# Another order for the first loads, the row products and the early FFN units of a causal attention and FFN kernel

## The chip, the cores and the metric

The kernel runs on one core of a Trainium2 chip. The metric is the device time of one execution in microseconds (us); lower is better. Engines: PE (TensorE), DVE (VectorE), ACT (ScalarE), POOL (GpSimd) and SP (SyncE), each with its own queue of instructions, which it works off in order. DMA transfers are issued from the queues of SP and POOL.

## The reference

Causal attention with 16 beacon keys that every query sees (8 batches, 8 heads, 576 tokens, head size 64), and on its output a multiplicative FFN with four weights.

```python
k_all = concat([beacon_k, k], axis=2); v_all = concat([beacon_v, v], axis=2)
scores = q @ k_all^T / sqrt(64)          # later tokens masked, beacons never
a = softmax(scores); x = (a @ v_all)     # -> 4608 tokens x 512
out = (((x @ w1) * (x @ w2)) @ w3) @ w_out      # d_ff = 1024
```

Inputs and output are float32.

## The kernel before, in words

All matmuls are in float16. `w3 @ w_out` is formed once, on the chip, into `Wt` (8 row blocks of 128 by 512), so the FFN is two matmul stages. The instructions stand in the order in which the program writes them; a framework adds the semaphores. A tile pool with `bufs=n` hands out n buffers in turn, and a new tile waits until all that used the old one in its buffer is done. On POOL's and on SP's queue a DMA also waits for the DMA that was issued eight before it on that queue.

**The head.** `load_first(a)` issues on SP, for a = 0 to 3, row block a of w3 and the matching 256 rows of w_out as float32 into a staging tile of pool `gp` (two buffers); `cast_first` turns them to float16, w3 on DVE and w_out on ACT. `w3_transposed(kt)` turns block kt on PE (8 transposes) and copies the result on DVE (`wT`). `fuse(acc, wT, r0, r1)` multiplies it with pieces r0 to r1 of w_out into an accumulator; pieces 2a and 2a+1 come from w_out load a. The accumulators of blocks 0 to 3 lie in the two `ps` tiles that the attention scores use afterwards. Blocks 4 to 7 follow in between the attention of batch 0: `row_first` (transposes), `row_a`, `row_b` (four fuses each) and a copy to `Wt` on ACT or DVE. `spin(n)` issues n matmuls on zeros.

**Loads.** `later_loads()` puts the other loads on POOL's queue, with a cast to float16 on the way: `load_pair(t)` (q and k of two heads of batch 0), `load_w3(4..7)`, `load_v(0, c)` (v of batch 0 in 5 chunks and the beacons), `load_w12` (w1 and w2), then q, k and v of batch 1. A memset on DVE at L144 comes ahead of the first of them, and the queue waits for it. `reorder_first(t)` (DVE) and `pe_transpose_first(t)` (PE, then DVE and ACT copies) make qT and kT of pair t, here T(t). Batch 1 is transposed on PE as well (`pe_transpose_second`). From batch 2 on, `transpose_qk(b, c)` does it by DMA transposes on SP, one for q and one for k of each of 5 chunks.

**Attention.** A step s is half of a head pair; 8 steps make a batch (`NSB`). `ahead(s)` is `scores(s)` and its two exps. `scores(s)` fills two `ps` tiles (pool `psS`, two buffers), `exps(s, j)` empties them on ACT, `masks` runs on DVE, `values(s)` multiplies with v, and DVE writes the normalised x. Batch 0 and 1 are put into `xT` by PE transposes (`pe_transpose_x`), later batches by DMA transposes on SP.

**The FFN** is a stream of units, one matmul of 128x512 each. A token tile of 512 has 96 units: 64 of `ff_ab` (groups of four; the first group of a pair is copied by ACT to `a_sb`, the second is multiplied with it by DVE) and 32 of `ff_out` (DVE, then a store on SP). `emit_ff(n)` puts n units into PE's queue. `marks` says how many units are out by which step:

```python
    for s in range(NSB, NS):
        ...
        values(s)
        ...
        k1 = min(4, fill[s])
        emit_ff(k1)
        if more:
            exps(s + 1, 1)
            mask(s + 1, 0)
        emit_ff(fill[s] - k1)
```

Here `scores(s + 1)` and `exps(s + 1, 0)` come ahead of `values(s)`, so that the second exp stands behind the first k1 units in the program.

Of the kernel before, what the change touches and what calls it, by code (L numbers as in the profile page):

```python
# [8 lines left out]
FP32 = mybir.dt.float32  # L9
# [3 lines left out]
ds, ts = bass.ds, bass.ts  # L13
# [26 lines left out]
def kernel(  # L40
# [13 lines left out]
    nc = tc.nc  # L54
# [78 lines left out]
    def load_pair(t):  # L133
        o16s[t] = []
        for i, (src, home) in enumerate(((q, q16s), (k, k16s))):

            flat = (
                home[0].rearrange("p c d -> p (c d)")[:NR, ds(t * RUN * P, RUN * P)]
                if t < 2
                else xT[:NR, 2 * (t - 2) + i, ds(2 * S, RUN * P)]  # L140
            )
            st = flat.rearrange("p (h x) -> p h x", h=2)
            if t == 0 and i == 0:
                nc.vector.memset(st[0:1, 0, 0:1], 0.0)  # L144
            nc.gpsimd.dma_start(
                st, src[0, ds(2 * t, 2)].rearrange("h (p j) d -> p h (j d)", j=RUN)
            )
            o16s[t].append(st)
        if t == 0:
            nc.gpsimd.dma_start(  # L150
                b16.rearrange("p (h d) -> p h d", h=H),
                beacon_k[0].rearrange("h n d -> n h d"),
            )
# [3 lines left out]
    def reorder_first(t):  # L157
        for i in range(2):
            o16 = tiny.tile([P, RUN, P], FP16, name=f"o16_{i}")
            nc.vector.tensor_copy(  # L160
                o16[:NR].rearrange("p j (h d) -> p h j d", h=2),
                o16s[t][i].rearrange("p h (j d) -> p h j d", j=RUN),
            )
            o16s[t][i] = o16

    def pe_transpose_first(t):
        qT, kT = qTs[0], kTs[0]
        for o16, dst, off, copy in (
            (o16s[t][0], qT, 0, nc.vector.tensor_copy),
            (o16s[t][1], kT, Nb, nc.scalar.copy),  # L170
        ):
            pt = psM.tile([P, 1024], FP16, name="pm")
            for j in range(RUN):
                nc.tensor.transpose(pt[:, ds(j * NR, NR)], o16[:NR, j, :], ident[:NR, :NR])
            if off:
                nc.tensor.transpose(pt[:, ds(S, Nb)], b16[:, ts(t, P)], ident[:Nb, :Nb])
                copy(dst[:, t, 0:Nb], pt[:, ds(S, Nb)])
            copy(
                dst[:, t, ds(off, S)].rearrange("p (i j) -> p i j", j=RUN),
                pt[:, 0:S].rearrange("p (j i) -> p i j", j=RUN),  # L180
            )
# [34 lines left out]
    def spin(n):  # L216
        pm = psM.tile([P, 512], FP32, name="pm")
        for _ in range(n):
            nc.tensor.matmul(pm, zeros[:, 0:P], zeros)  # L219
# [15 lines left out]
    def load_w3(kt):  # L235
        nc.gpsimd.dma_start(w316[:, kt // 2, kt % 2], moe_w3[ts(kt, P), :])
# [6 lines left out]
            )  # L243


    firsts = []

    def load_first(a):
        st = gp.tile([P, 2, 2 * DM], FP32, name="gT")
        nc.sync.dma_start(st[:, 0, :], moe_w3[ts(a, P), :])  # L250
        nc.sync.dma_start(
            st[:, 1, :],
            moe_w_out[ds(a * 2 * P, 2 * P), :].rearrange("(p c) n -> p (c n)", c=2),
        )
        firsts.append(st)

    def cast_first(a, i):
        if i == 0:
            nc.vector.tensor_copy(w316[:, a // 2, a % 2], firsts[a][:, 0, :])
        else:  # L260
            nc.scalar.copy(
                wo16[:, ds(2 * a, 2), :].rearrange("p c n -> p (c n)"), firsts[a][:, 1, :]
            )

    load_first(0)
    load_first(1)
    nc.gpsimd.affine_select(
        ident,
        ident,
# [25 lines left out]
    def later_loads():  # L295
        load_pair(0)
        load_w3(4)
        load_pair(1)
        load_w3(5)
        for c in range(NJT):  # L300
            load_v(0, c)
        load_pair(2)
        load_w3(6)
        load_pair(3)
        load_w3(7)
        load_w12(0)
        load_w12(1)
        for c in range(NJT):
            load_q(1, c)
            load_k(1, c)  # L310
        for c in range(NJT):
            load_v(1, c)


    def w3_transposed(kt):
        pt = psM.tile([P, NFT, P], FP16, name="pm")
        for rt in range(NFT):
            nc.tensor.transpose(
                pt[:, rt, :],
                w316[:, kt // 2, kt % 2, ds((rt // 2) * 2 * P, 2 * P)].rearrange(  # L320
                    "p (x c) -> p c x", c=2
                )[:, rt % 2, :],
                ident,
            )
        wT = wp.tile([P, NFT, P], FP16, name="wT")
        nc.vector.tensor_copy(wT, pt)  # L326
        return wT

    def fuse(acc, wT, r0, r1):
        for rt in range(r0, r1):  # L330
            nc.tensor.matmul(  # L331
                acc,
                wT[:, rt, :],
                wo16[:, rt, :],
                start=(rt == 0),
                stop=(rt == NFT - 1),
            )
# [51 lines left out]
    def emit_ff(n):  # L389
        nonlocal emitted  # L390
        for _ in range(n):
            try:
                next(ff)
            except StopIteration:
                return
            emitted += 1
# [83 lines left out]
    n_first = 4  # L480
    fill = [0] * NS

    marks = [(NSB, 52), (2 * NSB, 96), (2 * NSB, 104), (26, 196), (58, 580), (NS, 652)]
    for (s0, u0), (s1, u1) in zip(marks, marks[1:]):
        for s in range(s0, s1):
            n = s1 - s0
# [2 lines left out]
    def ahead(s):  # L489
        scores(s)  # L490
        for j in range(2):
            exps(s, j)

    def masks(s):
        for j in range(2):
            mask(s, j)
# [4 lines left out]
    grow = [psS.tile([P, 2, 512], FP32, name="ps") for _ in range(2)]  # L501
    accs = [grow[kt // 2][:, kt % 2, :] for kt in range(4)]
    wTs = []
    for a in range(4):
        cast_first(a, 0)
        wTs.append(w3_transposed(a))
        cast_first(a, 1)
        if a < 2:
            load_first(a + 2)
        if a == 1:  # L510
            later_loads()
        if a:
            for kt in range(a):
                fuse(accs[kt], wTs[kt], 2 * a - 2, 2 * a)
            spin(1)
            fuse(accs[a], wTs[a], 0, 2 * a)
        else:
            spin(5)
    for kt in range(4):
        fuse(accs[kt], wTs[kt], NFT - 2, NFT)  # L520
    reorder_first(0)
    for kt in range(4):
        copy = nc.vector.tensor_copy if kt % 2 else nc.scalar.copy
        copy(Wt[:, kt, :], accs[kt])

    rows = {}

    def row_first(kt):
        wT = w3_transposed(kt)
        rows[kt] = (wT, psM.tile([P, DM], FP32, name="pm"))  # L530

    def row_a(kt):
        fuse(rows[kt][1], rows[kt][0], 0, 4)

    def row_b(kt):
        fuse(rows[kt][1], rows[kt][0], 4, NFT)
        copy = nc.scalar.copy if kt < 6 else nc.vector.tensor_copy
        copy(Wt[:, kt, :], rows[kt][1])

    pe_transpose_first(0)  # L540
    spin(3)
    ahead(0)
    reorder_first(1)
    pe_transpose_first(1)
    row_first(4)
    ahead(1)
    row_a(4)
    masks(0)
    ahead(2)
    reorder_first(2)  # L550
    pe_transpose_first(2)
    row_b(4)
    masks(1)
    row_first(5)
    ahead(3)
    row_a(5)
    masks(2)
    values(0)
    ahead(4)
    reorder_first(3)  # L560
    pe_transpose_first(3)
    row_b(5)
    masks(3)
    values(1)
    row_first(6)
    ahead(5)
    row_a(6)
    values(2)
    masks(4)
    ahead(6)  # L570
    for c in range(NJT):
        load_q(2, c)
        load_k(2, c)
    row_b(6)
    values(3)
    masks(5)
    row_first(7)
    ahead(7)
    values(4)
    masks(6)  # L580
    row_a(7)
    values(5)
    row_b(7)
    values(6)
# [2 lines left out]
    for c in range(NJT):  # L587
        load_v(2, c)
    pe_transpose_x(0)
    emit_ff(40)  # L590
    pe_transpose_second(0)
    emit_ff(4)
    pe_transpose_second(1)
# [4 lines left out]
    for s in range(NSB, NS):  # L598
        b, r = s // NSB, s % NSB
        more = s + 1 < NS and s + 1 != 2 * NSB  # L600
        if more:
            scores(s + 1)
            exps(s + 1, 0)
        values(s)
        if b == 1 and r % 2 == 0 and r < NSB - 4:
            pe_transpose_second(r // 2 + 2)
# [7 lines that stand above are left out]
            mask(s + 1, 1)  # L614
        if s == 2 * NSB - 1:
            pe_transpose_x(1)
            ahead(s + 1)
            emit_ff(8)
            masks(s + 1)
        if 1 <= b < B - 1:  # L620
            if r == (0 if b > 1 else 3):
                for c in range(NJT if b > 1 else 0):
                    load_v(b + 1, c)
                for c in range(NJT if b + 2 < B else 0):
                    load_q(b + 2, c)
                    load_k(b + 2, c)
            if 1 <= r <= NJT:
                transpose_qk(b + 1, r - 1)
    emit_ff(1 << 30)
# [28 lines left out]
```

## Time and profile before

| | |
|---|---|
| median of 6 runs | 317.92 us (315.68 to 323.82) |
| profiled execution | 317.32 us, span 315.6 us |
| clock of TensorE | 1.00 of full speed |
| PE busy | 293.8 us, 93% of the span |
| DVE, ACT, POOL busy | 165.6, 160.0, 114.8 us |
| first FFN matmul | 49.73 us after the span's start |

The span runs from the first to the last instruction; the time has some 1.7 us around it. In the profile's lines L12 is line 12 of the kernel; a group reads engine, operation, output <- input. A line of the list of waits reads: engine, tile and line that waited <- what ended the wait: us in total, times, longest. A line in order of time reads: start, duration (first to last of a run of alike instructions), engine, line, operation, shape, count, and in brackets the idle time ahead of it with its releaser.

### The profile page before, as it was taken

What the parts mean: (1) busy time and instruction counts of PE and PEld (TensorE: products, weight loads), DVE (VectorE), ACT (ScalarE), POOL (GpSimd) and SP (SyncE); (2) the same over time, 40 slices, a digit from 0 to 9 for tenths busy, and PEclk for the clock granted to TensorE, in tenths of its full rate; (3) what the DMA queues carried; (4) which work ended last, traced back from release to release, by engine and by line L of the source; (5) the groups of instructions that cost most, each with busy time, mean ns of one, the idle gap of its engine ahead of it and who ended that gap; (6) DMA issues with size and microseconds to landing.
All of it is one profiled execution on the core that took longest, in us unless ns stands there. A gap on an engine that the chain in (4) does not pass through costs nothing.

```text
span 315.6 us, 6971 instructions
## 1 busy us (share of the span) xinstructions
PE 293.8 (93%) x2813; PEld 150.6 (48%) x2813; DVE 165.6 (52%) x383; ACT 160.0 (51%) x225; POOL 114.8 (36%) x155
## 2 busy tenths in 40 slices
PE   8897878989879997999999999999999999999995
PEld 3353554445535453555554555455455554444442
DVE  4554674446635663556555555555555554434342
ACT  2347733476457763664566456745655661230320
POOL 4669359939484149306910871050000000000000
PEclk9999999999999999999999999999999999999999
DMA  7999999999999999999999999998434003402003
GB/s 261 305 169 184 205 160 131 119 155 90 144 216 141 157 114 158 184 140 116 205 168 145 118 226 154 135 120 187 92 67 134 28 2 67 143 0 100 33 2 133
DMA packets 162048, 42.67 MB, mean 135 GB/s; under 512 B 152288, under 2 KB 155872, under 8 KB 162016
## 3 DMA queue, kind: packets, MB, share of 16 engines
q0 software_dynamic: 109792, 17.57, 78.5%
q1 hardware_dynamic: 52224, 24.66, 40.6%
q8 instruction: 22, 0.36, 0.5%
q14 instruction: 10, 0.08, 0.1%
HBM read 39.32 MB, written 9.44 MB: 154 GB/s over the span
## 4 chain that ended last, share of the span: by engine, by line
PE 68%; DMA 17%; POOL 5%; DVE 4%; issue 3%; ACT 2%; SPq 0%; DVEq 0%; POOLq 0%
PE pm L346 33%; PE pm L367 14%; PE pv L454 9%; PE ps L412 6%; DMA k<-in_k_dram 5%; DMA qT<-q 3%; DMA xT<-in_moe_w_dram 3%; DMA xT<-x 2%; DMA kT<-k 2%; PE pm L331 2%; PE pm L219 2%; POOL q L103 1%; DMA xT<-in_k_dram 1%; ACT pT L421 1%; DVE wT L326 1%
## 5 line engine op out<-in xcount | busy, mean ns | idle before, releaser
L346 PE MATMUL pm<-xT,w 128*128 128x512 f16 x576 | 132.1, 379 | 2.8 <-DMA xT<-x 2.1
L421 ACT ACTIVATE pT<-ps 128x736 f16<-128x736 f32 (+3 forms) x128 | 105.3, 864 | 38.3 <-PE ps L412 37.9
L346 PEld LDWEIGHTS <-w 128*128 128x128 f16 x576 | 53.8, 98 | 62.6 <-issue 3.9
L357 ACT ACTIVATE a_sb<-pm 128x512 f32<-128x512 f32 x72 | 43.0, 597 | 79.3 <-PE pm L346 78.9
L359 DVE TENSOR_TENSOR gT<-pm,a_sb 128x512 f16<-128x512 f32 x72 | 49.8, 692 | 52.0 <-PE pm L346 51.9
L367 PE MATMUL pm<-Wt,gT 128*128 128x512 f16 x288 | 66.2, 379 | 0.1
L112 POOL DMA_DIRECT2D va<-in_v_dram x40 | 33.9, 860 | 58.5 <-PE pv L454 55.7
L454 PE MATMUL pv<-va,pT 128*128 128x65 f16 x912 | 41.3, 194 | 1.6 <-DVE pT L433 1.5
L454 PEld LDWEIGHTS <-pT 128*128 128x128 f16 x960 | 34.3, 97 | 14.3 <-issue 5.4
L412 PE MATMUL ps<-qT,kT 64*128 64x80 f16 (+3 forms) x704 | 36.2, 228 | 5.0 <-DMA qT<-q 1.6
L367 PEld LDWEIGHTS <-gT 128*128 128x128 f16 x288 | 26.7, 98 | 29.1 <-issue 0.4
L462 DVE RECIPROCAL rd<-pv 128x4 f32<-128x4 f32 (+1 forms) x62 | 11.7, 189 | 49.7 <-PE pv L454 49.6
L377 DVE TENSOR_SCALAR ot<-pm 128x512 f32<-128x512 f32 x36 | 24.9, 691 | 23.0 <-PE pm L367 22.9
L103 POOL DMA_DIRECT2D q<-in_q_dram x35 | 30.4, 870 | 16.6 <-DMA k<-in_k_dram 4.3
L412 PEld LDWEIGHTS <-kT 64*128 64x128 f16 x704 | 20.6, 95 | 32.2 <-issue 27.4
L112 POOL DMA_DIRECT2D k<-in_k_dram x35 | 30.3, 865 | 9.8 <-DMA q<-in_q_dram 4.4
L463 DVE TENSOR_TENSOR x<-pv,rd 128x256 f16<-128x256 f32 (+1 forms) x62 | 30.3, 489 | 2.4
L433 DVE TENSOR_TENSOR pT<-pT,MB 128x512 f16<-128x512 f16 x64 | 20.1, 324 | 0.2 <-ACT pT L421 0.2
L433 DVE TENSOR_TENSOR pT<-pT,MA 128x480 f16<-128x480 f16 x32 | 12.8, 399 | 0.3 <-ACT pT L421 0.3
L219 PE MATMUL pm<-zeros 128*128 128x512 f16 x25 | 9.0, 502 | 1.3 <-DVE zeros L214 1.3
L331 PE MATMUL pm<-wo,wT 128*128 128x512 f16 x32 | 8.3, 381 | 1.8 <-DVE wT L326 1.7
L331 PEld LDWEIGHTS <-wT 128*128 128x128 f16 x64 | 5.4, 98 | 7.9 <-DVE wT L326 2.5
(62 smaller groups left out, 104.1 us busy)
## 6 DMA issues: line engine op xcount, KB each, us to landing
out_dram<-ot SPq DMA_DIRECT2D x36, 256.0 KB, 4.0
q<-in_q_dram POOLq DMA_DIRECT2D x28, 128.0 KB, 10.3
va<-in_v_dram POOLq DMA_DIRECT2D x24, 128.0 KB, 6.2
k<-in_k_dram POOLq DMA_DIRECT2D x21, 128.0 KB, 11.5
gT<-in_moe_w_dram SPq DMA_DIRECT2D x4, 512.0 KB, 3.6
gT<-in_moe_w_out_dram SPq DMA_DIRECT2D x4, 512.0 KB, 4.4
w<-in_moe_w_dram POOLq DMA_DIRECT2D x4, 512.0 KB, 11.2
xT<-in_moe_w_dram POOLq DMA_DIRECT2D x4, 256.0 KB, 6.3
```

The costliest lines, as they stand in the source:

```text
L103: nc.gpsimd.dma_start(q16s[b % NB2][:rows, c, :].rearrange("s (h d) -> s h d", h=H), q[b, :, ds(c * P, rows), :].rearrange("h s d -> s h d"),)
L112: nc.gpsimd.dma_start(dst[ds(p0, rows)], src[b, :, ds(s0, rows), :].rearrange("h s d -> s h d"))
L346: nc.tensor.matmul(pm, w12[:, kt, ds(i * DF + kf * P, P)], xT[:, kt, ds(mc * 512, 512)], start=(kt == 0), stop=(kt == NKT - 1),)
L357: nc.scalar.activation(a_sb, pm, AF.Copy, scale=GS)
L359: nc.vector.tensor_tensor(gT[:, kf, :], pm, a_sb, ALU.mult)
L367: nc.tensor.matmul(pm, gT[:, kf, ts(mt, P)], Wt[:, kf, :], start=(kf == 0), stop=(kf == NFT - 1),)
L377: nc.vector.tensor_scalar(ot, pm, float(1.0 / GS), None, ALU.mult)
L412: nc.tensor.matmul(ps[:, hh, ds(col, n)], kT[ds(hh * 64, 64), t, ts(jt, P)], qT[ds(hh * 64, 64), t, ds(q0, n)],)
L421: nc.scalar.activation(pT[:, :, ds(GO[g], GW[g])], pss[s][j][:, :, 0 : GW[g]], AF.Exp, scale=scale)
L433: nc.vector.tensor_tensor(blk, blk, m.unsqueeze(1).to_broadcast([P, 2, n]), ALU.mult)
L454: nc.tensor.matmul(pv[:, 2 * n + hh, 0:65], pT[:, hh, ds(col, P)], va[:, jt, 2 * t + hh, 0:65], start=(jn == 0), stop=(jn == len(BLK[i]) - 1),
L463: nc.vector.tensor_tensor(x16[:, ds(tiles[0], ni), ds(t * P, P)].rearrange("p i (h d) -> p i h d", h=2), pv[:, 0 : 2 * ni, 0:64].rearrange ...
```

## The change

- The first loads and casts are ordered w3(0), w_out(0), w3(1), w_out(1), w3(2), w3(3), w_out(2), w_out(3). A staging tile holds two w3 blocks or two w_out blocks, not one of each. The cast of a w_out load is shared: one half on ACT, one on DVE. Fuses and spins are ordered accordingly, and pair 0's transposes stand ahead of the last eight fuses.
- In `later_loads`, batch 0's v loads go behind pair 2, and the seventh w3 block behind pair 3.
- The row products of batch 0 stand in another order; `row_first` is now `row_t`, with the accumulator taken in `row_a`; the copies of blocks 4 to 6 are on DVE and that of block 7 is on ACT.
- Ahead of batch 1 there are 52 FFN units, not 40; the marks are 64 units (52 before) at step 8 and 192 at step 27 (196 at step 26).
- The ten DMA transposes of batch 2 are queued on SP right after those 52 units, ahead of any store; before, they were queued in steps 9 to 13, with a store after the second chunk and after the fourth.

```diff
+    firsts = {}
+    def load_first(i, a):
+        if a % 2 == 0 and i == 0:
+            firsts[a // 2] = [gp.tile([P, 2, 2 * DM], FP32, name="gT") for _ in range(2)]
+        st = firsts[a // 2][i][:, a % 2, :]
         ...
+    def cast_first(i, a):
+        st = firsts[a // 2][i][:, a % 2, :]
+        if i == 0:
+            nc.vector.tensor_copy(w316[:, a // 2, a % 2], st)
+        else:
+            nc.scalar.copy(wo16[:, 2 * a, :], st[:, 0:DM])
+            nc.vector.tensor_copy(wo16[:, 2 * a + 1, :], st[:, DM:])
+    for a in range(2):
+        for i in range(2):
+            load_first(i, a)
     ...
         load_w3(5)
+        load_pair(2)
         for c in range(NJT):
             load_v(0, c)
-        load_pair(2)
+        load_pair(3)
         load_w3(6)
-        load_pair(3)
         load_w3(7)
     ...
-    marks = [(NSB, 52), (2 * NSB, 96), (2 * NSB, 104), (26, 196), (58, 580), (NS, 652)]
+    marks = [(NSB, 64), (2 * NSB, 96), (2 * NSB, 104), (27, 192), (58, 580), (NS, 652)]
     ...
+    cast_first(0, 0)
+    wTs.append(w3_transposed(0))
+    spin(5)
+    cast_first(1, 0)
+    cast_first(0, 1)
+    load_first(0, 2)
+    load_first(0, 3)
+    wTs.append(w3_transposed(1))
+    fuse(accs[0], wTs[0], 0, 2)
+    spin(1)
+    cast_first(1, 1)
+    load_first(1, 2)
+    load_first(1, 3)
+    later_loads()
+    fuse(accs[1], wTs[1], 0, 2)
+    fuse(accs[0], wTs[0], 2, 4)
+    fuse(accs[1], wTs[1], 2, 4)
+    for a in (2, 3):
+        cast_first(0, a)
+        wTs.append(w3_transposed(a))
+        spin(3)
+        fuse(accs[a], wTs[a], 0, 4)
+    for a in (2, 3):
+        cast_first(1, a)
+        if a == 3:
+            reorder_first(0)
+            pe_transpose_first(0)
+        for kt in range(4):
+            fuse(accs[kt], wTs[kt], 2 * a, 2 * a + 2)
     ...                              # copies of accs to Wt, as before
+    ahead(0); reorder_first(1); pe_transpose_first(1)
+    row_t(4); ahead(1); row_a(4); masks(0); ahead(2); row_b(4); masks(1)
+    row_t(5); reorder_first(2); pe_transpose_first(2); row_a(5); ahead(3)
+    row_b(5); masks(2); ahead(4); values(0); masks(3); values(1); ahead(5)
+    masks(4); values(2); reorder_first(3); pe_transpose_first(3); row_t(6)
+    values(3); row_a(6); ahead(6); ...; row_b(6); masks(5); row_t(7)
+    values(4); ahead(7); row_a(7); masks(6); values(5); row_b(7); values(6)
     ...
-    emit_ff(40)
+    emit_ff(52)
+    for c in range(NJT):
+        transpose_qk(2, c)
     ...
-            if 1 <= r <= NJT:
+            if b > 1 and 1 <= r <= NJT:
                 transpose_qk(b + 1, r - 1)
```

In the list of calls above, several lines of the program stand on one line.

More of the change, by code (lines that the diff above doesn't have):

```diff
@@ L243, in load_w12 @@
             )
[L246 to L257, printed above, removed]
+    firsts = {}
[3 more added lines that the diff above has]
+        st = firsts[a // 2][i][:, a % 2, :]
         if i == 0:
-            nc.vector.tensor_copy(w316[:, a // 2, a % 2], firsts[a][:, 0, :])
+            nc.sync.dma_start(st, moe_w3[ts(a, P), :])
         else:
-            nc.scalar.copy(
-                wo16[:, ds(2 * a, 2), :].rearrange("p c n -> p (c n)"), firsts[a][:, 1, :]
-            )
-    load_first(0)
-    load_first(1)
+            nc.sync.dma_start(
+                st,
+                moe_w_out[ds(a * 2 * P, 2 * P), :].rearrange("(p c) n -> p (c n)", c=2),
+            )
+    def cast_first(i, a):
[8 more added lines that the diff above has]
+            load_first(i, a)
     nc.gpsimd.affine_select(
@@ L503 @@
     wTs = []
-    for a in range(4):
-        cast_first(a, 0)
-        wTs.append(w3_transposed(a))
[L507 to L521, printed above, removed]
+    cast_first(0, 0)
[17 more added lines that the diff above has]
+        cast_first(0, a)
+        wTs.append(w3_transposed(a))
+        spin(3)
[7 more added lines that the diff above has]
+            fuse(accs[kt], wTs[kt], 2 * a, 2 * a + 2)
     for kt in range(4):
@@ L526, with row_t @@
     rows = {}
-    def row_first(kt):
-        wT = w3_transposed(kt)
-        rows[kt] = (wT, psM.tile([P, DM], FP32, name="pm"))
+    def row_t(kt):
+        rows[kt] = [w3_transposed(kt)]
     def row_a(kt):
+        rows[kt].append(psM.tile([P, DM], FP32, name="pm"))
         fuse(rows[kt][1], rows[kt][0], 0, 4)
@@ L536, in row_b @@
         fuse(rows[kt][1], rows[kt][0], 4, NFT)
-        copy = nc.scalar.copy if kt < 6 else nc.vector.tensor_copy
+        copy = nc.scalar.copy if kt > 6 else nc.vector.tensor_copy
         copy(Wt[:, kt, :], rows[kt][1])
-    pe_transpose_first(0)
-    spin(3)
     ahead(0)
@@ L544 @@
     pe_transpose_first(1)
-    row_first(4)
+    row_t(4)
     ahead(1)
@@ L549 @@
     ahead(2)
+    row_b(4)
+    masks(1)
+    row_t(5)
     reorder_first(2)
     pe_transpose_first(2)
-    row_b(4)
-    masks(1)
-    row_first(5)
+    row_a(5)
     ahead(3)
-    row_a(5)
+    row_b(5)
     masks(2)
+    ahead(4)
     values(0)
-    ahead(4)
+    masks(3)
+    values(1)
+    ahead(5)
+    masks(4)
+    values(2)
     reorder_first(3)
     pe_transpose_first(3)
[L562 to L566, printed above, removed]
+    row_t(6)
+    values(3)
     row_a(6)
-    values(2)
-    masks(4)
     ahead(6)
@@ L574 @@
     row_b(6)
-    values(3)
     masks(5)
-    row_first(7)
+    row_t(7)
+    values(4)
     ahead(7)
-    values(4)
+    row_a(7)
     masks(6)
-    row_a(7)
     values(5)
```

## The prediction

> **What bounds the kernel now.** I read the page first, then PE's waits, then PE, SP, ACT and DVE in order of time.
>
> ```profile
> span 315.6 us, 6971 instructions
> PE 293.8 (93%) x2813; PEld 150.6 (48%) x2813; DVE 165.6 (52%) x383; ACT 160.0 (51%) x225; POOL 114.8 (36%) x155
> ```
>
> TensorE is busy for 293.8 of 315.6 us and every matmul stays, so only idle time of PE can be won: 21.8 us. PE's waits by releaser, from the list of waits:
>
> ```profile
> PE pm L346 <- DMA xT<-x: 2.1, 1, 2.1
> PE pm L174 <- DVE o L160: 2.1, 3, 1.1
> PE pm L331 <- DVE wT L326: 1.7, 3, 0.7
> PE ps L412 <- DMA qT<-q: 1.6, 2, 1.2
> PE ps L412 <- ACT pT L421: 1.4, 4, 0.7
> PE ps L412 <- DMA kT<-k: 1.1, 1, 1.1
> ```
>
> In order of time, PE idles in the head up to the first FFN matmul at 49.73 us (6.3 us of listed gaps from 21.5 on), some 2 us in batch 1 (62 to 86), and at three places that the change aims at:
>
> ```profile
> 88.69 0.39 PE L412 MATMUL ps<-qT,kT 64*128 64x256 f16 x4 [1.20 <-DMA qT<-q]
> 92.29 0.35 PE L412 MATMUL ps<-qT,kT 64*128 64x80 f16 x10 [1.10 <-DMA kT<-k]
> 124.16 1.02 PE L346 MATMUL pm<-xT,w 128*128 128x512 f16 x4 [2.13 <-DMA xT<-x]
> ```
>
> From 125 on only two gaps are listed (0.39 at 203, 0.67 at 263). What moves PE earlier before 125 therefore reaches the end.
>
> **Part 1, batch 2's transposes: -2.3.** SP before, in order of time:
>
> ```profile
> 60.27 1.89 SPq L128 DMA_TRANSPOSE kT<-k  x1
> 76.44 0.34 SPq L378 DMA_DIRECT2D out_dram<-ot  x1
> 76.88 1.29 SPq L127 DMA_TRANSPOSE qT<-q  x1
> ```
>
> SP stood from 62 to 76 because the first store sat ahead of the third pair of transposes and its tile was ready only at 76.4; the last kT transpose was issued at 85.20 and landed at 92.24. The loads they need were done far earlier: POOL's wait for the load of k's fourth chunk of batch 2 ended at 66.9, the fifth is the next one. Behind no store, the last pair goes out near 72 (ten issues of about 1.3 us, in step with the loads) and lands by 80 at the 7.3 us that such a transpose takes. PE asks for it at about 88. Both waits go, 1.20 + 1.10. The four stores now queue behind ten transposes, but their tiles are made after 75, so nothing waits for them. Bounds: 0 and -2.3.
>
> **Part 2, the FFN units moved by the marks.** One unit is 0.216 us of PE (12 in 2.59). Twelve units move from batch 1 to before it, which costs nothing: PE does them anyway. Batch 1 then has 4 units a step, all from the second FFN matmul, and no a_sb copy on ACT. Its idle gaps were 0.18, 0.68, 0.22 and 0.62. The 0.68 goes (it ends an a_sb of 0.60 between two exps), but with fewer units PE waits about 0.45 at each of the two steps where ACT has two exps and a 0.69 kT copy (2.85 us against 2.4 of PE work). I take -0.5, bounds -1.5 and +0.6.
>
> Mark (26,196) becomes (27,192): the third FFN tile, which reads batch 2's xT, starts two steps later. Two steps of 8 units are over 5 us of PE work and it was 2.13 late: **-2.1**, bounds 0 and -2.1. Steps 27 to 57 then have 12.5 units for 12, which adds 0.9 us before the wait at 203 (0.39): **-0.2**, bounds -0.4 and +0.4.
>
> The price: steps 16 to 26 have 8 units, not 9.2. PSUM tiles ps come in twos, so the second half of the next scores must wait for the second exp of this step. In ACT's queue of the changed kernel an a_sb stands between the two exps of each of the steps 16 to 22, and it needs four FFN matmuls. Before, two steps look like that:
>
> ```profile
> 93.83 0.60 ACT L357 ACTIVATE a_sb<-pm 128x512 f32<-128x512 f32 x1 [1.79 <-PE pm L346]
> 94.33 1.64 ACT L421 ACTIVATE pT<-ps 128x800 f16<-128x800 f32 x2
> 94.81 0.80 PE L412 MATMUL ps<-qT,kT 64*128 64x128 f16 x8
> 97.62 1.89 ACT L421 ACTIVATE pT<-ps 128x1024 f16<-128x1024 f32 x2
> 98.31 0.73 PE L412 MATMUL ps<-qT,kT 64*128 64x128 f16 x14
> ```
>
> Scores of 8 and 14 matmuls took 0.80 and 0.73 where others take 0.55 and 0.52: PE stalled between halves, with 9 units. From one second half to the next it was 92.29 to 95.21, 2.92 us, set by ACT; with 8 units PE needs 0.3 + 0.2 + 1.73 + 0.27 = 2.5. For an odd step ACT's chain is 3.7 (3.48 measured with three units ahead of the a_sb, here four), PE's 3.06. Four even steps at 0.4 and three odd ones at 0.6 make 3.4; 0.3 was there before. I take **+3.0**, bounds 0 (the later 9-unit steps, whose scores took 0.55 and 0.52) and +3.5.
>
> **Part 3, the head: +1.4.** The staging tile of the first pair now holds w3(0) and w3(1), so the load of w3(2) waits for the cast of w3(1), which stands behind the first wT copy and a new half cast of w_out on DVE.
>
> ```profile
> 6.63 0.33 SPq L250 DMA_DIRECT2D gT<-in_moe_w_dram  x1
> 7.51 0.69 DVE L326 COPY wT<-pm 128x1024 f16<-128x1024 f16 x1 [2.28 <-PE pm L318]
> 8.12 0.68 DVE L259 CAST xT<-gT 128x1024 f16<-128x1024 f32 x1
> 10.40 0.69 DVE L259 CAST xT<-gT 128x1024 f16<-128x1024 f32 x1 [0.19 <-DMA gT<-in_moe_w_dram]
> ```
>
> 8.20 (copy) + 0.35 (half of a 0.68 cast) + 0.68 = 9.23, where SP issued it at 6.63. The first load took 0.82 to 4.33, 3.5 us: it lands at 12.75, not 10.40. From there DVE and PE alternate: cast to 13.43, transposes 0.62 and copy 0.69 to 14.8, cast of w3(3) to 15.5, transposes and copy to 17.05 (before: 15.66). The w_out loads, issued at 11.05 and 11.5 at 4.3 us each, are in by then, and q and k of pair 0 too (POOL starts 0.9 later, since its gate, the memset of L144, stands behind another half cast). PE then runs 4 + 8 fuses, 13 transposes, 8 fuses: 0.87 + 1.74 + 0.75 + 1.74, to 22.15. Before, fuses and transposes were done at 19.98, but three spins and the qT copy held scores(0) to 21.53. Now the Wt copies, in turn on ACT (0.59, behind 0.8 of kT) and DVE (0.69), free the two ps tiles at 22.6 and 23.3; the first exps end near 24.6 for 23.6, +1.0.
>
> After that pair 2 is no longer late (its loads pass six v loads; they landed at 26.8 and 27.5 and are now needed near 30), which takes away 1.12 + 0.30. But T(2) stands behind a DVE chain: row_b(4) ends at 28.0, then Wt(4), which is DVE's now, 0.62, masks(1) 0.5, wT(5) 0.62, reorder 0.35: 30.1, with PE idle for some 1.7 from the end of row_t(5). The v loads, moved back by two DMAs, are first read at about 34 (31.6 before), pair 3 at 38 (33.1). Walking on with the same rows, PE waits for DVE at values(1) 0.6, T(3) 1.0, row_a(7) 0.6, and 1.2 at values(7) for masks(7), as before (1.42). FFN starts near 51.1, not 49.73. Bounds: -1.0 (the weights land as before and the old waits for DVE go) and +3.5 (the Wt copies on DVE delay every row). Half casts leave ACT (1.04 to about 0.6 each), where they hid behind loads anyway; the one spin more, 0.22, lies under a DVE copy. w12 lands about 1 later (43.7 before), still before 51; q and k of batch 1 landed near 55 and are asked for at 62.
>
> [...]
>
> **Sum.** +1.4 - 0.5 - 2.3 + 3.0 - 2.1 - 0.2 = -0.7. The profiled execution took 317.32 (span 315.6 and 1.7 around it), so 316.6. It lay 0.6 below the median of 317.92, so I give 317.2. Gains at three waits are spent on ACT and in the head.
>
> **Rivals.** *ACT keeps up* in steps 16 to 22: that term is 0 and the time 314.2, 1.2% faster. For it: most 9-unit steps show no stall. Against: the two with the same queue order do. *The transposes are late anyway*, since they share the DMA engines with POOL's loads (engine share 2.46 in 60 to 65 us): +2.3, 319.5. Against: 8 us to spare. *Slower, by one mechanism:* the third w3 load, now in flight as POOL's stream starts, lands as slowly as the w12 loads do beside it (8.1 us at least, not 3.5): everything from the 12.75 on moves by 4.6, to 321.8. It decides beyond 1% from a landing at about 16.7. Against: w3(3), 3.4 us beside POOL.
>
> **How the numbers follow.** Forecast 0.46 (315.0 to 319.5), ACT keeps up 0.30, late transposes 0.08, slow third weight 0.16. One per cent, 3.2 us, is about what a measurement of this kernel can tell from no change. Below 314.7 lie 0.24 of the second case and 0.03 of the forecast; above 321.1 lie 0.13 of the last, 0.05 of the forecast and 0.02 of late transposes: 0.27, 0.53, 0.20. The range, 312.5 to 322.0, takes ACT's bound together with part of the head's, and the late weight.
>
> **What would show it.** Right: w3(2) issued past 9 us; first FFN matmul past 50.5; the last kT transpose landed before 82 and no DMA wait at scores(16) and (17); no wait for xT near 124; gaps of 0.3 to 0.6 with ACT as releaser at every step from 16 to 22. The forecast is wrong if the FFN starts before 49.5, if those steps show no gap, or if a wait for a DMA appears after 60 us.

## The result and the profile after

| | before | changed |
|---|---|---|
| median | 319.52 us (67 runs) | 321.93 us (30 runs) |
| ratio, 95% interval | | 1.0107 (1.0089 to 1.0125) |
| profiled execution | 317.32 us, span 315.6 | 323.77 us, span 322.1 |
| its mean granted clock | 1.000 | 0.989 |
| at full clock (below) | 316.9 +- 0.3 us | 320.1 +- 0.3 us |

The medians lie 2.4 us apart, where -0.7 was forecast. The ratio is higher than they make it, since it leaves out the slow runs, those more than 1.5% above the fastest of their kernel, which only the kernel before has here. The page of the changed kernel, its first lines and its row of clocks:

```profile
span 322.1 us, 6968 instructions
PE 295.1 (92%) x2814; PEld 150.6 (47%) x2814; DVE 167.2 (52%) x388; ACT 157.5 (49%) x224; POOL 115.6 (36%) x155
PEclk9999899999999999997999999999999999999999
```

In the row of clocks there are dips, which the profiled execution of the kernel before does not have: TensorE ran at half clock for two short stretches (31.8 to 35.2 and 147.9 to 151.3 us). In this execution they stand behind stretches in which PE had little to do. PE's windows of 2 us around them (bounds, length, PE busy and its matmuls, clock, DMA share, GB/s):

```profile
28.00:30.00 2.00, 0.46 (x9) 1.00 1.11 125
30.00:32.00 2.00, 1.68 (x17) 0.95 1.03 168
32.00:34.00 2.00, 2.00 (x18) 0.50 1.20 204
144.00:146.00 2.00, 0.35 (x5) 1.00 1.77 155
146.00:148.00 2.00, 1.39 (x30) 0.96 1.74 158
148.00:150.00 2.00, 2.00 (x6) 0.50 1.11 197
```

Other executions of the same kernel have a mean clock of up to 1.000, and those of the kernel before go from 0.979 to 1.000. Its profiled execution did not dip, though PE idled 2.13 us at 122 us:

```profile
122.00:124.00 2.00, 0.03 (x1) 1.00 2.28 157
124.00:126.00 2.00, 1.84 (x26) 1.00 1.71 247
```

So the clock is a noise of its own, and it has to be taken out before differences of 1 us mean anything. Each execution comes with its mean granted clock. A least-squares fit over every execution of every kernel here (one constant for each kernel, one common slope) gives 2.95 +- 0.23 us for each per cent of clock that is missing; a dip of 3.4 us at half clock, as these two are, is by an estimate from these numbers about half a per cent of the mean clock, 1.5 us. The mean clock was 0.991 before and 0.994 after, so the kernel before lost 2.7 us to it on average and the changed one 1.8. "At full clock" in this text is the constant of that fit, with its 95% interval. The expectations quote figures of the same fit made before the last four runs, when the slope was 2.97 or 2.98. At full clock the change costs **+3.2 +- 0.45 us**.

PE's list of waits, after (engine, tile, line, what ended the wait: total, times, longest):

```profile
PE ps L416 <- ACT pT L425: 3.9, 10, 0.6
PE pv L458 <- DVE pT L437: 3.4, 5, 0.8
PE pm L174 <- DVE o L160: 3.1, 3, 1.9
PE ps L416 <- DMA qT<-q: 2.9, 2, 2.3
```

Before, ACT's exps held up scores four times for 1.4 us, and xT's DMA came first; here the exps lead with ten waits, and xT is gone from the top. PE in order of time, after:

```profile
23.06 0.40 PE L416 MATMUL ps<-qT,kT 64*128 64x256 f16 x4 [0.53 <-DVE Wt L539]
30.32 0.69 PE L174 MATMUL pm<-ident,o 96*128 96x96 f16 x12 [1.86 <-DVE o L160]
53.44 11.38 PE L350 MATMUL pm<-xT,w 128*128 128x512 f16 x52 [0.53 <-ACT xT L208]
...
91.84 0.55 PE L416 MATMUL ps<-qT,kT 64*128 64x128 f16 x8
95.58 0.36 PE L458 MATMUL pv<-va,pT 128*128 128x65 f16 x6 [0.80 <-DVE pT L437]
98.21 0.39 PE L416 MATMUL ps<-qT,kT 64*128 64x256 f16 x4 [0.28 <-ACT pT L425]
101.91 0.35 PE L416 MATMUL ps<-qT,kT 64*128 64x80 f16 x10 [0.47 <-ACT pT L425]
...
130.33 2.75 PE L350 MATMUL pm<-xT,w 128*128 128x512 f16 x12
146.61 0.40 PE L416 MATMUL ps<-qT,kT 64*128 64x256 f16 x4 [2.26 <-DMA qT<-q]
```

Four things are to be seen. The first FFN matmul comes at 53.44, not 49.73 (with a dip, some 1.5 us, ahead of it). At 91.84 scores(16) no longer waits for qT or kT. From 98 to 118 each step has a gap behind an exp. And at 130.33 xT is in time, but scores(32) waits 2.26 us for the transposes of batch 4, where the kernel before had no wait. SP's queue in order of time shows why:

```profile
8.65 0.81 SPq L253 DMA_DIRECT2D gT<-in_moe_w_dram  x2
71.19 1.21 SPq L128 DMA_TRANSPOSE kT<-k  x1
...
125.00 2.71 SPq L382 DMA_DIRECT2D out_dram<-ot  x3
127.82 1.30 SPq L127 DMA_TRANSPOSE qT<-q  x1
131.08 0.52 SPq L382 DMA_DIRECT2D out_dram<-ot  x1
```

The third w3 load goes out at 8.65, and batch 2's last transpose at 71.19 (85.20 before). Batch 4's first transpose went out at 127.82, and at 123.63 before, each time right behind three stores of the second FFN tile. The last of the three cannot go before DVE has written its tile. SP and that write before, and the write after:

```profile
120.24 2.88 SPq L378 DMA_DIRECT2D out_dram<-ot  x3
123.63 1.32 SPq L127 DMA_TRANSPOSE qT<-q  x1
122.07 0.69 DVE L377 TENSOR_SCALAR ot<-pm 128x512 f32<-128x512 f32 x1 [0.19 <-PE pm L367]
126.65 0.69 DVE L381 TENSOR_SCALAR ot<-pm 128x512 f32<-128x512 f32 x1 [0.62 <-PE pm L371]
```

The tile was ready at 122.76 before and is ready at 127.34 now. It is late for two reasons: scores(25) starts 4.3 us later, and with 8 units a step the second tile's units come out later in the program, so that its fourth store now stands behind the first pair of batch 4's transposes (131.08). At the same time PE, no longer held by xT, needs only 23.08 us from scores(25) to scores(32) (120.94 to 144.02), where it needed 26.58 before (116.67 to 143.25).

### The profile page after: what moved, and what is told of

The parts are those of the page before. It is cut to its first block, busy times and chain, and to the rows that moved or that the text cites. A ratio compares the mean times of both kernels' runs of the same rounds, so it can differ in the third digit from the quotient of the medians.

```text
span 322.1 us, 6968 instructions
## 1 busy us (share of the span) xinstructions
PE 295.1 (92%) x2814; PEld 150.6 (47%) x2814; DVE 167.2 (52%) x388; ACT 157.5 (49%) x224; POOL 115.6 (36%) x155
## 4 chain that ended last, share of the span: by engine, by line
PE 61%; DMA 17%; DVE 6%; POOL 5%; ACT 5%; issue 3%; SPq 1%; DVEq 0%; POOLq 0%
PE pm L350 29%; PE pm L371 14%; PE pv L458 8%; DMA qT<-q 5%; PE ps L416 5%; ACT pT L425 3%; DMA k<-in_k_dram 3%; DMA xT<-in_moe_w_dram 3%; DMA q<-in_q_dram 2%; PE pm L335 2%; DMA gT<-in_moe_w_dram 2%; POOL va L112 2%; ACT a_sb L361 1%; DVE pT L437 1%; DVE ot L381 1%
## 5 line engine op out<-in xcount | busy, mean ns | idle before, releaser
L371 PE MATMUL pm<-Wt,gT 128*128 128x512 f16 x288 | 66.9, 379 | 0.0
L112 POOL DMA_DIRECT2D va<-in_v_dram x40 | 33.9, 859 | 66.3 <-PE pv L458 62.2
L416 PE MATMUL ps<-qT,kT 64*128 64x80 f16 (+3 forms) x704 | 37.0, 231 | 7.8 <-ACT pT L425 3.9
L458 PE MATMUL pv<-va,pT 128*128 128x65 f16 x912 | 39.4, 194 | 4.7 <-DVE pT L437 3.4
L458 PEld LDWEIGHTS <-pT 128*128 128x128 f16 x960 | 33.3, 97 | 15.6 <-DVE pT L437 5.5
L335 PE MATMUL pm<-wo,wT 128*128 128x512 f16 x32 | 9.3, 417 | 1.2 <-DVE wT L330 1.1
L219 PE MATMUL pm<-zeros 128*128 128x512 f16 x26 | 8.0, 452 | 1.3 <-DVE zeros L214 1.3
```

The lines of the kernel that those rows point to most:

```text
L112: nc.gpsimd.dma_start(dst[ds(p0, rows)], src[b, :, ds(s0, rows), :].rearrange("h s d -> s h d"))
L371: nc.tensor.matmul(pm, gT[:, kf, ts(mt, P)], Wt[:, kf, :], start=(kf == 0), stop=(kf == NFT - 1),)
L416: nc.tensor.matmul(ps[:, hh, ds(col, n)], kT[ds(hh * 64, 64), t, ts(jt, P)], qT[ds(hh * 64, 64), t, ds(q0, n)],)
L458: nc.tensor.matmul(pv[:, 2 * n + hh, 0:65], pT[:, hh, ds(col, P)], va[:, jt, 2 * t + hh, 0:65], start=(jn == 0), stop=(jn == len(BLK[i]) - 1),
```

## The experiments

All were timed in five rounds beside the kernel before; medians in us, the ratio to the kernel before with its 95% interval, and the difference at full clock. First the parts of the change, each put into the kernel before.

**Head alone** (loads, first stage, `later_loads`, row order).

```diff
 # kernel before, with the changed load_first, cast_first, first stage,
 # later_loads and row order; the marks and transposes stay
```

> The kernel before with the changed head alone (order of the first loads, fuses and row products; v behind pair 2); units, marks and transposes as before. Theory A (ledger of the two traces: head +3.7 us in the first FFN matmul, 1.6 of it a stretch at half clock): first FFN matmul near 53.4 and about 3 to 4 us slower than before (+1.0 to +1.2%). Rival B (the head's loss is absorbed, since batch 1 and 2 wait for DMAs that arrive at their own time: the qT and kT waits of 2.3 us shrink): slower by 1.5 us at most.

323.59, 1.0051 (0.9996 to 1.0106); at full clock +3.2 +- 0.6. The interval of the ratio touches 1, since this kernel and the one before differ in their dips too, but at full clock the head is as dear as the whole change.

**First loads and first stage alone**, with the old `later_loads` and rows:

> The kernel before with the changed order of the first eight weight loads, their staging tiles, split casts, fuses and spins alone; row products, v loads and all later as before. Theory A (the late load of w3(2) and the Wt copies that pair 0's exps then wait for cost 1.0 at the first exps, and this runs through): first FFN matmul 50.7 to 51.0 (49.73 before), 1.0 to 1.3 slower at full clock. Rival B (the load of pair 2 comes at its own time, so a later start is absorbed): first FFN matmul by 50.0, same time.

319.50, 1.0031 (0.9995 to 1.0067); +1.2 +- 0.6. PE in order of time, at scores(0):

```profile
22.93 0.39 PE L416 MATMUL ps<-qT,kT 64*128 64x256 f16 x4 [0.53 <-DVE Wt L539]
```

scores(0) now needs both `ps` tiles emptied by the Wt copies: its second half stands at 22.93, where the old stage had both halves out from 21.53 on.

**Row order and v loads alone**, behind the old first stage:

```diff
+        load_pair(2)
         for c in range(NJT):
             load_v(0, c)
-        load_pair(2)
+        load_pair(3)
 ...                     # row_t, row_a, row_b and T(2), T(3) in the new order
-        copy = nc.scalar.copy if kt < 6 else nc.vector.tensor_copy
+        copy = nc.scalar.copy if kt > 6 else nc.vector.tensor_copy
```

> The kernel before with the changed order of row products 4 to 7 (copies of 4 to 6 on DVE), v loads behind pair 2 and the seventh w3 block behind pair 3 alone. Theory A (PE waits for DVE's chain of copy, masks, copy, reorder ahead of T(2), and again at values(1), T(3) and row_a(7)): 1.5 to 2.0 slower at full clock, with DVE as the releaser of 1.5 us or more ahead of T(2). Rival B (the loss in the head is all from the late weights, and the DVE chain only fills the time that they cost): same time or faster, as pair 2's wait of 1.42 is gone.

322.40, 1.0101 (1.0053 to 1.0149); +1.4 +- 0.8, with a mean clock of 0.986, the lowest of all. PE in order of time has the long wait of T(2) without the new loads:

```profile
29.82 0.69 PE L174 MATMUL pm<-ident,o 96*128 96x96 f16 x12 [2.13 <-DVE o L160]
```

The two halves of the head, 1.2 and 1.4, come within their errors to its 3.2.

**Batch 2's transposes alone.**

```diff
     emit_ff(40)
+    for c in range(NJT):
+        transpose_qk(2, c)
...
-            if 1 <= r <= NJT:
+            if b > 1 and 1 <= r <= NJT:
```

> The kernel before with the ten DMA transposes of batch 2 queued right after the 40 units, ahead of any store, and nothing else. Theory A: the two waits at scores(16) and (17) go, 2.3 us faster (-0.7%). Rival B (earlier transposes slow POOL's loads of batches 1 to 3, so PE waits elsewhere): no gain or a wait for a DMA elsewhere between 56 and 115 us.

315.95, 0.9883 (0.9829 to 0.9936); -1.4 +- 0.8. The good part of the change. Both waits for DMAs at scores(16) and (17) are gone, but PE's order of time has a new one behind them, and the wait for xT is longer:

```profile
90.24 0.35 PE L454 MATMUL pv<-va,pT 128*128 128x65 f16 x6 [0.80 <-DVE pT L433]
122.16 1.83 PE L346 MATMUL pm<-xT,w 128*128 128x512 f16 x4 [2.47 <-DMA xT<-x]
```

Of the 2.30 that went, 0.80 came back at once: without the DMA's wait, values(16) asks for a mask that is not made yet. Another 0.34 came back at xT (2.47 for 2.13). By these lists some 1.2 is left, and 1.4 +- 0.8 by the runs.

**52 units ahead of batch 1 alone.**

```diff
-    marks = [(NSB, 52), (2 * NSB, 96), ...
+    marks = [(NSB, 64), (2 * NSB, 96), ...
-    emit_ff(40)
+    emit_ff(52)
```

> The kernel before with 52 FFN units ahead of batch 1 and mark 64 alone (four units a step in batch 1, not 5.5). At full clock (a run's time less 2.97 us for each 1% that its mean granted clock lies under 1, the slope of the runs so far) the kernel before takes 317.2, the changed one 320.0. Theory A (the parts add up: head +2.8, transposes -1.8, mark 27 +0.2, so 1.6 is left for this one): 1.0 to 2.0 slower than before at full clock, with waits of values for masks of about 0.65 in batch 1. Rival B (my prediction): 0.5 faster. Rival C (the rest is an interaction of parts): no difference.

322.58, 1.0083 (1.0043 to 1.0123); +2.1 +- 0.7. PE in order of time:

```profile
78.50 0.35 PE L454 MATMUL pv<-va,pT 128*128 128x65 f16 x6 [0.65 <-DVE pT L433]
92.23 0.61 PE L412 MATMUL ps<-qT,kT 64*128 64x256 f16 x4 [4.21 <-DMA qT<-q]
```

Three times in batch 1 values lose 0.65, as they come sooner than their masks. And batch 2's transposes are late by 4.21, not 1.20. SP in order of time shows why:

```profile
72.34 0.35 SPq L378 DMA_DIRECT2D out_dram<-ot  x1
72.80 1.30 SPq L127 DMA_TRANSPOSE qT<-q  x1
```

With 12 units more ahead of batch 1, the first tile's first store is ready sooner (72.34, not 76.44), but it comes two steps sooner in the program too, and now stands ahead of all ten transposes. Before, it stood behind the first four, which went out from 56.10 on; here none goes out before 72.80, and the last one goes out at 88.67, not 85.20.

**The same with the transposes ahead of the stores**, to part these two: the two edits above together.

> The kernel before with batch 2's transposes ahead of the stores and 52 units ahead of batch 1 (mark 64), nothing else. Times are compared at full clock, that is with 2.98 us taken off for each per cent of mean granted clock that is missing; the kernel with the transposes alone stands at 315.4 there. Theory: the four units taken out of the steps of batch 1 leave its values waiting for their masks (0.65 us at three or four places, as in the run of the 52 units alone), so it costs about 1.0: 316.4. Rival 1: the loss of the 52 units alone (1.8) was only the longer block of stores ahead of batch 2's transposes, which is gone here: 315.4, no change. Rival 2, the prediction's term: -0.5, so 314.9.

316.82, 0.9950 (0.9914 to 0.9987); -1.4 +- 0.6 at full clock, and 0.0 +- 0.9 against the transposes alone. The waits of 0.65 at the masks are there (74.58, 80.39 and 84.90), and from the first FFN matmul to the last transposes of batch 1's x (51.18 to 88.81) it is 37.63 us, 0.98 longer than in the run of the transposes alone (36.65). So the first rival fits the times, and the theory fits the trace; the errors hold 0 to 0.9. The loss that is shown for certain is the one to the stores, and the change does not have it.

**The third mark alone.**

```diff
-    marks = [..., (2 * NSB, 104), (26, 196), ...
+    marks = [..., (2 * NSB, 104), (27, 192), ...
```

> The kernel before with the mark (26,196) moved to (27,192) alone. Theory A: the xT wait near 124 (2.13) goes, but ACT holds PE at each of steps 16 to 22 (+3.0), and the slower stores of the second FFN tile hold back batch 4's transposes on SP, so that scores(32) waits some 2 us for qT, with a stretch at half clock behind it: 2 to 5 us slower (+0.6 to +1.5%). Rival B (my prediction's sum for this part): +0.7, no wait at scores(32).

319.51, 0.9949 (0.9906 to 0.9992); +0.6 +- 0.6 at full clock, where the ratio is a little below 1: a gain in the medians that the clock explains as well. The xT wait goes, the gaps of 0.28 and 0.47 come at scores(18) to (24), and scores(32) waits:

```profile
146.34 0.40 PE L412 MATMUL ps<-qT,kT 64*128 64x256 f16 x4 [2.00 <-DMA qT<-q]
```

So this wait comes with the mark alone; no kernel here without the mark waits for a DMA at scores(32). The trace puts the mark's cost higher than the runs do: from the second half of scores(17) to the end, with no dip in it, the execution takes 225.4 us, and that of the kernel before 223.3.

**Filling T(2)'s gap**, in the changed kernel:

```diff
     row_t(5)
     reorder_first(2)
+    spin(7)
     pe_transpose_first(2)
```

> The changed kernel with seven spins (matmuls on zeros, 1.5 us) between row_t(5) and T(2), where PE idles 1.86 us and the granted clock then falls to half for 3.4 us. Theory A (the idle stretch trips the clock): the clock stays 1.00 there, first FFN matmul 1.5 earlier, 1 to 1.7 us faster than the changed kernel. Rival B (the clock falls for another reason, such as the sparse head as a whole): same time and the same stretch at half clock.

322.93, 1.0090 (1.0057 to 1.0123); +0.9 +- 0.6 against the changed kernel, with the same mean clock (0.994). The gap ahead of T(2) fell to 0.63, but the profiled execution has a dip later in the head, and its first FFN matmul stands at 54.24:

```profile
38.00:40.00 2.00, 0.84 (x17) 1.00 1.22 200
40.00:42.00 2.00, 2.00 (x39) 0.69 1.43 197
42.00:44.00 2.00, 2.00 (x12) 0.50 2.36 154
```

The longest gap listed ahead of this dip, from 31.3 on, is 1.00 us, at T(3). Filling the gap at T(2) does not buy the clock.

**Wt copies back on ACT**, in the changed kernel:

```diff
-        copy = nc.scalar.copy if kt > 6 else nc.vector.tensor_copy
+        copy = nc.scalar.copy if kt != 6 else nc.vector.tensor_copy
```

> The changed kernel with the copies of three more transposed blocks of the weights moved from the VectorE to the ScalarE, so that the VectorE comes to the o of T(2) sooner. Theory: the wait of T(2) for o falls from 1.86 to about 1.2 us, 0.5 to 1 us off the time: 319.0 to 319.5 at full clock. Rival: the masks of step 1 and the copy of wT hold the VectorE whatever the Wt copies do: wait and time stay within 0.3 of 1.86 and 320.0.

The edit moves two copies, of blocks 4 and 5, and not three; block 7's was on ACT already. 320.56, 1.0105 (1.0069 to 1.0140); -0.6 +- 0.6 against the changed kernel. The wait fell about as the theory said:

```profile
30.43 0.70 PE L174 MATMUL pm<-ident,o 96*128 96x96 f16 x12 [1.05 <-DVE o L160]
```

1.05 for 1.86. The DVE chain ahead of T(2) is real, and what was taken from it is worth about as much, a small part of the head's 3.2; the error is as large as the gain. This profiled execution had a clock of 0.999, and its first FFN matmul stood at 52.05.

**Twelve units ahead of step 16**, in the changed kernel, which puts the copy of a_sb behind both exps:

```diff
-    marks = [..., (2 * NSB, 104), (27, 192), ...
+    marks = [..., (2 * NSB, 108), (26, 188), (27, 192), ...
...
-            emit_ff(8)
+            emit_ff(12)
```

> The changed kernel with 12 units ahead of step 16 instead of 8, and all later marks of the steps with 8 units moved by the four. The copy of a_sb then stands behind both exps of a step and not between them. Theory: the gaps of 0.28 and 0.47 us at scores that wait for an exp (2.5 us in sum) go, and 2.5 to 3.5 us with them: about 317 at full clock, where the changed kernel stands at 320.0. Rival: the gain in the kernel before with transposes ahead and 12 units came from the xT wait or the clock, and the gaps only move: within 0.7 of 320.0.

317.19, 0.9985 (0.9948 to 1.0022); **-4.3 +- 0.6** against the changed kernel. This one edit takes away more than the whole loss. PE and ACT in order of time, first the changed kernel, then this one, over like steps:

```profile
100.34 0.60 ACT L361 ACTIVATE a_sb<-pm 128x512 f32<-128x512 f32 x1 [1.51 <-PE pm L350]
100.84 1.72 ACT L425 ACTIVATE pT<-ps 128x1024 f16<-128x1024 f32 x2
101.10 0.34 PE L416 MATMUL ps<-qT,kT 64*128 64x128 f16 x4
101.91 0.35 PE L416 MATMUL ps<-qT,kT 64*128 64x80 f16 x10 [0.47 <-ACT pT L425]
```

```profile
101.26 0.52 PE L416 MATMUL ps<-qT,kT 64*128 64x128 f16 x14
101.36 0.60 ACT L361 ACTIVATE a_sb<-pm 128x512 f32<-128x512 f32 x1 [0.86 <-PE pm L350]
101.86 1.53 ACT L425 ACTIVATE pT<-ps 128x768 f16<-128x768 f32 x2
```

In the first, ACT idles 1.51 us until four FFN matmuls have made the input of a_sb; only then comes the second exp of the step, which empties the `ps` tile that the next scores need. In the second the copy comes after it, and the 14 matmuls of the scores run through. In the changed kernel two steps take 6.61 us (101.91 to 108.52), here 5.51 (101.26 to 106.77), with 16 units each. The listed gaps are only 0.28 + 0.47 = 0.75 of the 1.10: around each gap the line of scores breaks in two and PE loses another 0.18 that no bracket lists (0.47 and 0.65 in all). The four units also put PE's next need for a mask off by 0.86 us, which ends the 0.80 at values(16). Once 0.86 us of work cannot hide seven stalls of 3.8 in sum, so it is the order that ends these.

**The same with the head and the units of before**: transposes ahead of the stores, and 12 units ahead of step 16.

> The kernel before with batch 2's transposes ahead of any store, mark (27,192), and 12 FFN units, not 8, ahead of step 16 (marks 108 at step 16, 188 at step 26), so that in steps 16 to 22 the a_sb copy stands behind both exps in ACT's queue, not between them. Theory A (the stall of 0.3 to 0.5 a step is the a_sb between the exps): no wait for ACT at the scores of steps 17 to 23, no wait for xT near 122; scores(32) still waits about 2 us for qT; 1.5 to 2.5 faster than the kernel with the transposes alone if that wait stays away, else 0 to 1 faster. Rival B (eight units are too few whatever the order): the same gaps with ACT as releaser.

312.45, 0.9791 (0.9735 to 0.9847); -5.1 +- 0.8. It is faster than the kernel before by about 2%. No gap behind an exp is left between 90 and 122 us, and no wait for xT. But scores(32) still waits:

```profile
138.00 0.40 PE L412 MATMUL ps<-qT,kT 64*128 64x256 f16 x4 [1.79 <-DMA qT<-q]
```

In the run above it waits 1.61. So of the changed kernel's 2.26 at this place only about a quarter goes with the slow steps; the rest comes with the mark. The distance in time to the run above, 4.0 +- 0.9, is the new head and the 52 units once more.

**And the later batches' transposes one step earlier.**

```diff
-            if b > 1 and 1 <= r <= NJT:
-                transpose_qk(b + 1, r - 1)
+            if b > 1 and r < NJT:
+                transpose_qk(b + 1, r)
```

> The kernel before with batch 2's transposes ahead of the stores, 12 units ahead of step 16, and the later batches' transposes queued one step earlier. Theory: what is left is the wait of scores(32) for qT (1.79 us), set by where the transposes stand behind the stores; a step earlier it falls below 1, and the time by 0.8 to 1.5 us from 311.7 at full clock: 310.2 to 310.9. Rival: the transposes are held by the stores ahead of them in the queue all the same: the wait stays within 0.3 of 1.79, and the time within 0.5 of 311.7.

311.79, 0.9810 (0.9761 to 0.9859); -5.6 +- 0.8, and -0.5 +- 1.0 against the run above. PE in order of time:

```profile
135.27 0.39 PE L412 MATMUL ps<-qT,kT 64*128 64x256 f16 x4 [0.89 <-ACT pT L421]
139.78 0.35 PE L412 MATMUL ps<-qT,kT 64*128 64x80 f16 x10 [0.42 <-DMA kT<-k]
```

The wait of 1.79 shrinks to 0.42, but PE waits 0.89 for an exp in its place. SP shows that a step earlier in the program was hardly earlier in time: batch 4's last transpose went out at 132.47 against 134.42, and this execution ran 1.8 ahead all along. It is the fastest version here, by a margin over the one before it that is not shown.

## Why the prediction was wrong

Worked at full clock, the change was forecast at -0.7 and is +3.2 +- 0.45. Two steps of the sum failed above all: the head was put at +1.4 and costs +3.2, and the transposes and the units moved ahead of batch 1 were put at -2.8 together and bring -1.4 +- 0.6, since the waits for masks behind them were put at nothing. By its own steps:

- **Batch 2's transposes, -2.3: size off.** The issue times were as predicted (last kT out at 71.19, "near 72"), and both DMA waits went. But nothing in the text asked what is late next: the mask of step 16 is, by 0.80. Alone the step brings -1.4 +- 0.8.
- **ACT in steps 16 to 22, +3.0: mechanism right, size off.** The gaps come seven times, as said, but at scores(18) to (24) and not at steps 16 to 22, as 0.28 and 0.47 in turn, four and three of them. At 0.47 and 0.65 in truth that is 3.8, less the 0.46 that the two slow scores of the kernel before lost (0.80 for 0.55, 0.73 for 0.52): 3.4. From scores(17) to scores(25) it is 26.68 us in the changed kernel and 22.06 with the copy behind both exps: 4.6, which is 3.8 and the 0.80 of the mask. The term lies inside its bounds, near the upper one, so the size is off by some 0.4.
- **xT, -2.1: right.** No wait near 124 (unit 192 at 130.33 has none).
- **Batch 4's transposes: the step that is missing.** The prediction walked SP's queue for batch 2 only. At scores(25) PE is 4.3 us behind the kernel before, and batch 4's first transpose is late by as much (127.82 for 123.63). Then PE makes good 3.5 of it, as xT no longer holds it, and comes to scores(32) while SP is still late: 2.26. The slow steps are not the main reason, since without them the wait is still 1.61 and 1.79: the wait for xT that the mark took away had covered this one. "If a wait for a DMA appears after 60 us" was the test, and it appeared. Its worth is less than its length, since another wait stands behind it (0.89 in the best version), and the mark alone, with xT's gain, ACT's gaps and this wait, is +0.6 +- 0.6.
- **Units moved ahead of batch 1, -0.5: wrong in sign.** Exp waits of 0.55 and 0.39 near 70 were foreseen ("about 0.45"; there is a third, of 0.39), but not that values would wait 0.65 for masks at three places, since the masks stand behind the later exps. Batch 1 takes 0.98 longer in the trace; in the runs, between 0 and 1 (0.0 +- 0.9).
- **The head, +1.4: size off, and the largest miss.** Point by point it went much as worked out: w3(2) issued at 8.65 (9.23 predicted, and "past 9 us" was its test) and on the chip at 12.0; scores(0) at 22.20 and 23.06 (22.6 and 23.3); T(2) waiting 1.86 (1.7) behind the DVE chain; T(3) 1.00 (1.0); row_a(7) 0.79 (0.6); values(1) 0.74 (0.6); values(7) 1.01 (1.2). Only values(2) waited 0.43 that was not in it. Yet the runs say +3.2 +- 0.6. The traces agree with the runs. With the old head, the first FFN matmul stands at 48.62 to 49.73 in the four executions that have no dip ahead of it, 49.2 in the mean. With the new head it stands at 53.44, 54.05, 54.24 and 54.72, each with one dip ahead; less 1.5 for the dip, an estimate, that is 52.6 in the mean, 3.4 later; the one execution without a dip, with a wait shortened, has it at 52.05. So the forecast of 51.1 was 1.5 too early, and the 49.73 of the one profile that was read was the latest of the four. A head read off a single execution was known to about 1 us, and the text gave it to 0.1. Which of its waits carry the rest was not resolved further than 1.2 for the loads and 1.4 for the rows: that stays open.
- **The clock: not in the sum.** The working took the profiled execution's 1.00 as the rule. That execution was free of dips; the mean of the kernel before was 0.991, worth 2.7 us. A median of six executions, 317.92, was also 1.6 below that of 67.

Errors by the runs: head +1.8; transposes and units together +1.4 (-2.8 forecast, -1.4 +- 0.6 in the run of both); the mark, which holds ACT, xT and the wait of scores(32), none (+0.7 forecast, +0.6 +- 0.6). Together that is 3.2, known to about 1, for a miss of 3.9 +- 0.45. That the mark's sum comes out is in part luck: ACT's term was a little too small, the wait of scores(32) was left out, and by the trace the mark costs 2.1.

The measured median, 321.93, lies just inside the range that was given (to 322.0). That speaks for the width of the range and not for the working: the change went the other way than forecast.

The rivals: *late transposes* fell with the issue at 71.19. *A slow third weight* fell too: it landed at 12.0, and its 321.8 is near the measured median by luck. The last w_out load, worked out to be in by 17.05, was hardly later: the casts that waited for it started at 17.15. What made the kernel slower was none of them but the forecast's own two costs, head and ACT, each larger than said, and its gains, which were spent in part at the waits behind them. *ACT keeps up* is what the 12 units ahead of step 16 make true.

What sends the clock down was not shown. A gap of 2.13 us had no dip behind it in one execution, and gaps of 1.86 and 2.26 had one in another. Those dips came behind stretches in which PE still had 0.35 to 0.46 us of work in 2 us; in the run with the spins a dip came behind no listed gap above 1.00, with 0.84 us of work in 2 us.

## What to carry to other kernels

When work is taken out of a loop step, look at the engine that feeds the next one, and at what stands between two instructions of its queue that both free a buffer: here one copy between two exps cost 3.8 us over seven steps, and moving it behind both, by four more units up front, won more than the change lost. A wait that is removed is worth its length less the wait that stands behind it: the 2.30 us of waits for batch 2's transposes brought 1.4 +- 0.8, with 0.80 and 0.34 of new waits behind them. And a store whose tile was not ready held the transfers queued after it (in the kernel before, SP issued nothing from 62.2 to 76.4 us), so an edit that moves stores, in time or in the queue, asks for a walk through that queue, batches later too. And before a difference of 1% is explained from two profiles, ask what clock each had (here a mean of 1.000 and 0.989 in the two that were profiled, at 2.95 us for a per cent).

## What was not expected of the hardware

- The granted clock fell to 0.50 for about 3.4 us after a 2-us stretch with PE busy for 0.35 to 0.46 us, and elsewhere after one with 0.84 us; the mean clock of the same kernel goes from 0.989 to 1.000 over its executions. One per cent of mean clock was worth 2.95 +- 0.23 us. With less idle time ahead of T(2) (1.86 to 0.63) there was still a dip, some 9 us later; in the run with twelve units ahead of step 16 it stood there too (40 to 43.5 us), without the spins and behind a gap of 2.12 at T(2) that no dip followed.
- A gap listed as 0.28 or 0.47 us on PE lengthened the step by 0.18 us more than the list says.
